# Small edits around the first LayerNorm and the first group of a fused attention and MLP layer

## The chip, the cores and the metric

The kernel runs on one core of one Trainium2 chip. The metric is the device time of one launch in microseconds (us). A core has five engines that run side by side and wait for one another on semaphores: TensorE (PE; its weight loads are shown apart as PEld), VectorE (DVE), ScalarE (ACT), GpSimd (POOL) and SyncE (SP), which here only issues DMAs.

## The reference

The layer is a pre-LayerNorm block on x of 2048 tokens by 576, in bfloat16. First a sliding, dilated attention with 32 heads of 18, where a token looks at itself and at the tokens 2, 4, ... 14 before it. Then an MLP, 576 to 4608 to 576. The MLP has a LayerNorm of its own on an input that was already normalized, so h passes two of them (the kernel folds both into one).

```python
def _A_ref(x, wqkv, wo):
    qkv = (x @ wqkv).reshape(B, S, 3, H, Dh) ...
    idx = pos[:, None] - off[None, :]        # off = 0, 2, .. 14
    logits = where(mask, einsum("bhsd,bhswd->bhsw", q, kg) * scale, -1e9)
    o = einsum("bhsw,bhswd->bhsd", softmax(logits), vg)
    return o.transpose(0, 2, 1, 3).reshape(B, S, D) @ wo
def _B_ref(x, w1, b1, w2, b2):
    return gelu(layernorm(x) @ w1 + b1) @ w2 + b2
h   = x + _A_ref(layernorm(x), A_wqkv, A_wo)
out = h + _B_ref(layernorm(h), B_w1, B_b1, B_w2, B_b2)
```

## The kernel before, in words

The 2048 tokens are 16 tiles of 128 rows. Row p of tile j is token 16p + j, so a window with a step of 2 stays among tiles of one parity, and a tile of earlier tokens is the same tile moved down by one row (a halo, read back from DRAM by `halo`, L335). Even tiles are treated first. The attention goes backwards, 14, 12, ... 0, then 15, 13, ... 1 (`ATT_ORDER`), and two neighbours in that order are a group: group 0 is tiles 14 and 12, group 1 is 10 and 8.

The order of each engine's work is written out by hand (`tc.manual_schedule`, L783): each engine executes its own instructions in the order of the program and waits where an operand isn't ready. Tables of calls say what follows which visit of TensorE.

- **Start** (L784 to L874). SP issues the loads of x and of the weights one after another. VectorE takes statistics of each tile and centres it (`ln1_even`, L834); the reciprocal root is a power on GpSimd (`ln_rstd`, L158). TensorE transposes the centred even tiles (`tr_x`, L265) with `transpose_in` (L177): products with an identity, for two halves of the rows, into two halves of a pair of banks. The 576 columns make four blocks of 128 and a rest of 64. The fifth block takes the last 128 columns. For LN1 that is enough, since other weights stand under it; for o and h (`twice`), the last 64 columns are transposed once more into the upper 64 rows, so that both halves of the fifth block hold them. That makes 12 products instead of 10. A copy turns the pair into xnT.
- **QKV stage** (L963). 24 visits of two products each (`visit`, L230, `phase`, L209). A phase does half of the contraction for each half of the array; before the second phase, a no-op on GpSimd (`marker`, L225) waits for the first one's last matmul, and the second phase waits for the no-op. Since GpSimd works in order, a marker is also held by whatever stands ahead of it there. ScalarE evacuates each product (`evac`, L308), from three pairs of banks in turn (`ring_pair`, L290). Odd tiles are normalized by ScalarE (`ln1_act`) and transposed by DMA through DRAM (`out_x`, `in_x`).
- **Attention** (L343 to L409) is VectorE's: products of q with eight shifted K tiles, a tree of adds, maximum, subtraction (`att_max`), exponential on ScalarE, and the same with V.
- **Output product and LN2.** o is transposed on TensorE for group 0 (`tr_o`, L422), by DMA for the others. `wo_duo` multiplies it with wo. `ln2_h` (L459) adds x on VectorE. For group 0 VectorE also takes the statistics (`ln2_more`), adds b2 (`add_b2`, L503) and works out the bias -mean * rstd (`ln2_bias`), and ScalarE normalizes (`ln2_hn`). For other groups ScalarE does all of it (`ln2_act`, `ln2_send`), b2 is put into x's place by a DMA (`put_b2`), and h is added to that by a DMA from GpSimd's queue (`accumulate_h`, L509). Their result is stored to DRAM and read back transposed (`ln2_in`, L497).
- **MLP** (L1005 on), group by group: `mlp1` with GELU on ScalarE, then `mlp2`. While group k is in the MLP, the attention of the next groups is on VectorE. Group 0's MLP starts when TensorE's last QKV visit is done. Inside group 0's `mlp2`, at rows 0 and 19 of its first tile (`ia[0]`, `ia[19]`), stand LN2 of group 1 and the scores of group 2.

The part around the table of calls that the change edits, in the kernel before:

```python
17: [c_(ln2, A[0]), c_(att_qk_a, A[2])],
18: [c_(ln2_rstd, A[0]), c_(add_b2, A[0]), c_(ln2_bias, A[0]), c_(halo, A[2], 1), c_(att_qk_add, A[2], ((0, 0, 9),))],
19: [c_(ln2, A[1])],
20: [c_(ln2_rstd, A[1]), c_(add_b2, A[1]), c_(ln2_bias, A[1]), c_(att_qk_rest, A[2], 0, 1)],
```

Of the kernel before, what the change touches and what calls it, by code (L numbers as in the profile page):

```python
# [17 lines left out]
def kernel(  # L18
# [69 lines left out]
    qp = qp_cm.__enter__()  # L88
    wq_sb = qp.tile([P, KF, 3 * D], BF16, name="wq_sb")
    wqh_sb = qp.tile([P, 3, D], BF16, name="wqh_sb")  # L90
    b2_bc = x_all[:, ODD[-1], :]

    kv_dram = dram.tile([NT, P + 1, 2, D], BF16, name="kv_dram")
    sync_dep = mybir.DependencyInfo(mybir.DependencyClass.Sync, mybir.DependencyReason.DATA)
# [46 lines left out]
    def ln_stats(srcs, tag, c1, c0, bufs, first=None, eps=True):  # L141
        n = len(srcs)
        pool = qp if tag.startswith("ln1") else sb
        stats = pool.tile([P, n, 2, nc.vector.BN_STATS_DIM], F32, tag=f"{tag}_stats", name=f"{tag}_stats", bufs=bufs)
        mv = pool.tile([P, n, nc.vector.BN_AGGR_DIM], F32, tag=f"{tag}_mv", name=f"{tag}_mv", bufs=bufs)
        for i, src in enumerate(srcs):
            for c in range(2):
                nc.vector.bn_stats(out=stats[:, i, c, :], in_=src[:, c * HALF:(c + 1) * HALF])  # L148
            nc.vector.bn_aggr(out=mv[:, i, :], in_=stats[:, i, :, :])
            if i == 0 and first is not None:  # L150
                first()
        if not eps:
            return mv, None
        veps = sb.tile([P, n], F32, tag=f"{tag}_veps", name=f"{tag}_veps", bufs=bufs)
        nc.vector.tensor_scalar(out=veps[:], in0=mv[:, :, 1], scalar1=c1, scalar2=c0, op0=ALU.mult, op1=ALU.add)  # L155
        return mv, veps
# [10 lines left out]
    def ln_bias(mean, rstd, tag, bufs):  # L167
        n = rstd.shape[1]
        nmr = sb.tile([P, n], F32, tag=f"{tag}_nmr", name=f"{tag}_nmr", bufs=bufs)
        nc.vector.scalar_tensor_tensor(out=nmr[:], in0=mean, scalar=-1.0, in1=rstd[:], op0=ALU.mult, op1=ALU.mult)  # L170
        return nmr
# [2 lines left out]
        nc.scalar.activation(out=dst, in_=src, func=ACT.Identity, scale=rstd, bias=nmr)  # L174


    def transpose_in(pair, src, twice=True):  # L177
        def turn(rows, kt, c):
            for r in range(2):
                block = src[half_rows(r), c:c + P if rows.start is None else D]  # L180
                nc.tensor.matmul(pair[rows, r, kt * HP:(kt + 1) * HP], lhsT=block, rhs=ident[half_rows(r), half_rows(r)],
                                 start=True, stop=True, skip_group_check=True)

        for kt in range(KT):
            turn(slice(None), kt, min(kt * P, D - P))
        if twice:
            turn(half_rows(0), KF, KF * P)
# [18 lines left out]
    def half_rows(r):  # L206
        return slice(r * HP, (r + 1) * HP)
# [56 lines left out]

    def tr_x(j, tag):  # L265
        pair = psum_pair(tag or "CAB"[(ring_pos[0] + 1) % 3], "xt_pt")
        transpose_in(pair, q_all[:, j, :], False)
        if EVEN.index(j) % 2 == 0:
            new_xnT(EVEN[EVEN.index(j):][:2])
        for k0, k1 in ((0, 2), (2, KT)) if j in EVEN[0:2] else ((0, KT),):  # L270
            copy = nc.vector.tensor_copy if j == EVEN[1] and k0 == 0 else nc.scalar.copy
            copy(**turned(xnT[j], pair, k0, k1))  # L272

    xd = [dram.tile([2, P, KT * P], BF16, name=f"xd{i}") for i in range(NT // 4)]

# [53 lines left out]
    def sides(js):  # L329
        return slice(side[js[0]], side[js[0]] + len(js))  # L330

    def logit_of(js):
        return logits[:, sides(js)]
# [27 lines left out]
            nc.vector.memset(out[0:1, j // 2 + 1:W, :], -1e9)  # L361

    def att_max(js):
        n, sl, lg = len(js), sides(js), logit_of(js)
        nc.vector.tensor_reduce(out=peak[:, sl], in_=lg.rearrange("p i w h -> p i h w"), axis=AX.X, op=ALU.max)
# [55 lines left out]

    def tr_o(j, tag):  # L422
        pair = psum_pair(tag, "o_pt")
        transpose_in(pair, q_all[:, j, :])
        nc.scalar.copy(**turned(new_oT(j), pair))

    def dma_tr_o(j):
# [24 lines left out]
    def x_of(j):  # L452
        return x_all[:, j - j % 2, :]
# [16 lines left out]

    def ln2_more(j):
        h = h_of[j]
        hn[j] = (h,) + ln_stats([h[:]], "ln2", 1.0 + EPS, EPS * EPS, 2)

    def ln2_act(j):
        h = h_of[j]
# [23 lines left out]
            tc.add_manual_dep(read[0], stored[0].name, sync_dep, reason="stores ahead of the transposes of LN2")  # L500
            stored[0] = None

    def add_b2(j):  # L503
        nc.vector.tensor_tensor(out=x_of(j), in0=h_of.pop(j)[:], in1=b2_bc, op=ALU.add)

    def put_b2(j):
        nc.sync.dma_start(out=x_of(j), in_=B_b2.partition_broadcast(P))

    def accumulate_h(j):  # L509
        ins = nc.gpsimd.dma_start(out=x_of(j), in_=h_of.pop(j)[:], accum_op=ALU.add).ins  # L510
        tc.add_manual_dep(ins, read[0].name, sync_dep, reason="behind the transposes of LN2")

    def ln2_rstd(j):
        h, mv, veps = hn[j]
# [2 lines left out]
    def ln2_bias(j):  # L517
        h, mv, rstd = hn[j]
        hn[j] = (h, rstd, ln_bias(mv[:, :, 0], rstd, "ln2", 2))

    def ln2_hn(j):
        h, rstd, nmr = hn[j]
# [8 lines left out]

    def tr_h(j, tag):
        pair = psum_pair(tag, "h_pt")
        transpose_in(pair, hn.pop(j)[:])
        nc.scalar.copy(**turned(hnT_slot(j), pair))

    def gelu_table():
# [143 lines left out]
    def c_(fn, *a):  # L681
        return lambda: fn(*a)
# [100 lines left out]
    with tc.manual_schedule(engines={ENG.PE, ENG.Activation, ENG.DVE, ENG.SP, ENG.Pool}):  # L783
# [9 lines left out]
        load_x(EVEN[3:4])  # L793
        load_wqkv(2, 2, KF)
        load_wqkv_tail(nc.sync, 2)
        for j in EVEN[4:8]:
            load(x_all[:, j:j + 2, :], x3[:, j:j + 2, :])
        load_x(ODD[0:2])
        load_x(ODD[2:4])
        load_wqkv(0, 0, 2)  # L800
        load_wqkv(0, 2, KF)
        load_wqkv_tail(nc.sync, 0)
# [113 lines left out]
        for n, v in enumerate((19, 19, 20, 20, 21, 22)):  # L916
# [3 lines left out]
            1: [c_(ln1_even_rstd, 2, 3), c_(ln1_even, 5)],  # L920
            2: [c_(ln1_even, 6), c_(ln1_even, 7), c_(ln1_even_rstd, 4, 5)],
            3: [c_(ln1_even_rstd, 6, 7), c_(ln1_stats, 8)],
            4: [c_(ln1_rstd, 8), c_(ln1_stats, 9), c_(ln1_stats, 10, c_(ln1_bias, 8))],
            5: [c_(ln1_act, 8, 0), c_(ln1_rstd, 9), c_(ln1_bias, 9), c_(att_qk_a, A[0])],
            6: [c_(ln1_rstd, 10), c_(ln1_act, 8, 1), c_(halo, A[0], 1), c_(out_x, 0)],
            7: [c_(att_qk_rest, A[0], 0), c_(ln1_bias, 10), c_(ln1_act, 8, 2), c_(in_x, 0)],
# [21 lines left out]
        wo_with = {17: A[0], 19: A[1]}  # L948
# [56 lines left out]
        for k, g in enumerate(GROUPS):  # L1005
# [123 lines left out]
```

## Time and profile before

| what | value |
|---|---|
| three runs of the kernel | 361.35, 362.5, 366.2 us (median 362.5) |
| the profiled execution: time, span | 361.35 us, 359.6 us |
| TensorE busy, granted clock | 353.4 us (98%), full |
| VectorE, ScalarE, GpSimd busy | 296.3, 234.8, 46.5 us |
| first transposes of x; first MLP matmul of group 0, of group 1 | 4.94; 66.55; 105.21 us |
| mean of a power for LN1 or LN2 statistics on GpSimd (L161) | 965 ns, 548 to 3007 |
| an accumulating DMA issued by GpSimd (L510) | 862 to 1547 ns of GpSimd |

The span is the profiled stretch of one execution; the time also has what lies around it. An engine is busy while an instruction runs on it. Matmuls are pipelined, so TensorE's busy time holds short stalls too; its waits and the distance of two starts say more. In a list of waits a row is "who waits <- for whom: total, times, longest", and a row of a timeline is start, length, engine, line, operation, output <- inputs, and in brackets the idle time ahead with what ended it.

### The profile page before, as it was taken

To read this page: it belongs to the slowest core of one execution; us is meant where nothing else is said; L and a number is where in the kernel's file an instruction comes from. 1 tells how busy PE (TensorE), PEld (TensorE's weight loads), DVE (VectorE), ACT (ScalarE), POOL (GpSimd) and SP (SyncE) were. 2 spreads that over 40 slices of the span, in tenths; PEclk is the share of its full clock that TensorE was granted. 3 is DMA by queue.
4 is the path that set the end of the run, shared out by engine and by line. 5 is a ranking of instruction groups with operands and counts; after the bars stand their busy time and mean duration, and the time that the engine had idled before them with its cause. 6 is when DMAs were issued, how large, how long until landed. Compare 5 with 4: busy or idle time off the path is not lost.

```text
span 359.6 us, 11560 instructions
## 1 busy us (share of the span) xinstructions
PE 353.4 (98%) x4942; PEld 292.4 (81%) x4942; DVE 296.3 (82%) x417; ACT 234.8 (65%) x519; POOL 46.5 (13%) x61
## 2 busy tenths in 40 slices
PE   7999999999999999999999999999999999999996
PEld 3778977887789877887788778877887788778874
DVE  5999999999989999997799899989998998520431
ACT  4879756897647783668566956695669566706620
POOL 2241004000112020201110202021102110210000
PEclk9999999999999999999999999999999999999999
DMA  7996789973447494731563655344636254273001
GB/s 241 339 285 192 202 223 300 369 246 73 136 88 119 142 239 81 137 71 51 94 101 76 98 124 85 90 96 110 88 90 100 57 86 58 54 122 50 4 1 33
DMA packets 62980, 46.29 MB, mean 129 GB/s; under 512 B 32192, under 2 KB 60736, under 8 KB 62928
## 3 DMA queue, kind: packets, MB, share of 16 engines
q1 hardware_dynamic: 58960, 41.50, 44.0%
q0 software_dynamic: 3744, 3.84, 9.8%
q8 instruction: 38, 0.62, 0.8%
q10 hardware_dynamic: 224, 0.22, 0.2%
q14 instruction: 14, 0.11, 0.1%
HBM read 23.38 MB, written 12.42 MB: 100 GB/s over the span
## 4 chain that ended last, share of the span: by engine, by line
PE 76%; DVE 14%; DMA 3%; SPq 2%; ACT 2%; issue 1%; POOL 0%; POOLq 0%; ACTq 0%
PE pm L216 34%; PE po L669 25%; PE pq L216 8%; PE po L581 5%; PE pw L216 4%; DVE prod L352 2%; DVE ln_stats L148 2%; DVE prod L343 2%; DVE prod L398 1%; DMA x_all<-in_A_x_dram 1%; DVE prod L404 1%; ACT h_all L562 1%; SPq L104 1%; DMA hnT<-td 1%; DMA oT<-td 1%
## 5 line engine op out<-in xcount | busy, mean ns | idle before, releaser
L216 PE MATMUL pm<-hnT,w_sb 64*128 64x256 bf16 x2304 | 143.0, 269 | 0.2 <-DMA hnT<-td 0.2
L562 ACT ACTIVATE h_all<-pm,b_sb 128x256 f16<-128x256 f32 (+1 forms) x288 | 108.6, 496 | 51.2 <-PE pm L216 50.6
L216 PEld LDWEIGHTS <-w_sb 64*128 64x128 bf16 x2304 | 113.6, 94 | 13.5 <-issue 1.9
L669 PEld LDWEIGHTS <-h_all 128*128 128x128 f16 x480 | 46.2, 98 | 13.7 <-issue 1.6
L216 PE MATMUL pq<-wq_sb,xnT 64*128 64x288 bf16 x720 | 54.9, 283 | 1.3 <-ACT xnT L272 0.5
L216 PEld LDWEIGHTS <-xnT 64*128 64x128 bf16 x864 | 44.0, 94 | 10.6 <-ACT xnT L272 1.2
L352 DVE TENSOR_TENSOR prod<-prod 128x2304 bf16<-128x2304 bf16 (+1 forms) x64 | 44.2, 691 | 2.0
L343 DVE TENSOR_TENSOR prod<-kv_ring,q_all 128x4608 bf16<-128x4608 bf16 x16 | 40.9, 2555 | 3.1 <-POOL ln_rstd L482 2.5
L398 DVE TENSOR_TENSOR prod<-kv_ring,probs 128x4608 bf16<-128x4608 bf16 x16 | 40.9, 2558 | 1.1 <-DMA kv_ring<-kv_dram 0.6
L216 PE MATMUL pm<-hnT,w1h_sb 64*128 64x256 bf16 x288 | 39.5, 269 | 0.0
L669 PE MATMUL po<-w2a_sb,h_all 128*128 128x288 bf16 (+1 forms) x262 | 35.8, 286 | 0.0
L404 DVE TENSOR_TENSOR prod<-prod 128x2304 bf16<-128x2304 bf16 (+1 forms) x32 | 33.9, 1058 | 1.1
L581 PEld LDWEIGHTS <-h_all 128*128 128x128 bf16 x288 | 27.9, 98 | 7.9 <-issue 1.0
L669 PEld LDWEIGHTS <-kv_ring 128*128 128x128 f16 x252 | 24.6, 98 | 6.3
L581 PE MATMUL po<-w2a_sb,h_all 128*128 128x288 bf16 x224 | 28.5, 286 | 0.0
L216 PE MATMUL pq<-wqh_sb,xnT 64*128 64x288 bf16 x144 | 27.6, 283 | 0.0
L771 POOL DMA_DIRECT2D x_all<-o_sb x12 | 10.7, 890 | 124.6 <-PE pw L216 71.8
L482 POOL TENSOR_TENSOR ln_rstd<-ln_var,mhalf 128x1 f32<-128x1 f32 x13 | 9.3, 718 | 81.9 <-ACT ln_var L481 81.9
L669 PE MATMUL po<-w2b_sb,h_all 128*128 128x288 bf16 (+1 forms) x122 | 19.7, 286 | 0.2 <-DVE h_all L649 0.2
L649 DVE TENSOR_TENSOR kv_ring<-h_all 128x1536 f16<-128x1536 f16 (+3 forms) x9 | 6.8, 761 | 15.6 <-ACT h_all L562 15.6
L216 PE MATMUL pw<-wo_sb,oT 64*128 64x288 bf16 x256 | 19.5, 283 | 0.1
L161 POOL TENSOR_TENSOR ln_rstd<-ln_veps,mhalf 128x1 f32<-128x1 f32 (+2 forms) x14 | 13.3, 965 | 47.6 <-DVE ln_veps L155 31.1
(107 smaller groups left out, 399.3 us busy)
## 6 DMA issues: line engine op xcount, KB each, us to landing
w_sb<-in_B_w_dram SPq DMA_DIRECT2D x6, 768.0 KB, 6.3
kv_ring<-kv_dram SPq DMA_DIRECT2D x28, 144.0 KB, 2.4
kv_dram<-kv_ring SPq DMA_DIRECT2D x13, 288.0 KB, 4.1
x_all<-in_B_b_dram SPq DMA_DIRECT2D x15, 144.0 KB, 3.7
w2a_sb<-in_B_w_dram SPq DMA_DIRECT2D x2, 1008.0 KB, 8.0
td<-q_all SPq DMA_DIRECT2D x14, 144.0 KB, 1.8
td<-hn SPq DMA_DIRECT2D x14, 144.0 KB, 1.8
x_all<-h POOLq DMA_DIRECT2D x14, 144.0 KB, 4.8
```

Source lines behind the costliest of these rows:

```text
L148: nc.vector.bn_stats(out=stats[:, i, c, :], in_=src[:, c * HALF:(c + 1) * HALF])
L161: nc.gpsimd.tensor_tensor(out=rstd[:], in0=veps[:], in1=mhalf[:].to_broadcast([P, n]), op=ALU.pow)
L216: last = nc.tensor.matmul(duo["g"][r ^ swap][i], lhsT=lhsT, rhs=rhs, start=(swap == 0 and i == 0 and kt == 0), stop=(swap == 1 and kt == K ...
L343: ins = nc.vector.tensor_tensor(out=prod[:], in0=k_ring[j % 2], in1=q_all[:, j, :].unsqueeze(1) .to_broadcast([P, W, D]), op=ALU.mult).ins
L352: nc.vector.tensor_tensor(out=prod[:, :, o * H:o * H + n], in0=prod[:, :, a * H:a * H + n], in1=prod[:, :, c * H:c * H + n], op=ALU.add)
L398: nc.vector.tensor_tensor(out=prod[:].rearrange("p w (d h) -> p w d h", h=H), in0=v_ring[j % 2].rearrange("p w (d h) -> p w d h", h=H), in ...
L404: nc.vector.tensor_tensor(out=prod[:, 0:n, :], in0=prod[:, 0:n, :], in1=prod[:, n:2 * n, :], op=ALU.add)
L482: ins = nc.gpsimd.tensor_tensor(out=rstd[:], in0=var[:], in1=mhalf[:], op=ALU.pow).ins
L562: pace[0] = nc.scalar.activation(out=hT(grp)[:, f, 0:N], in_=ps[:, r, i * N:(i + 1) * N], func=ACT.Gelu_apprx_tanh, bias=b1_sb[:, f:f + 1] ...
L581: nc.tensor.matmul(banks[half], lhsT=hT(grp)[:, f, i * P:(i + 1) * P], rhs=w2_rows(f)[:, half * HALF:(half + 1) * HALF], start=(f == 0), s ...
L669: nc.tensor.matmul(bank, lhsT=l, rhs=r, start=start, stop=stop, skip_group_check=True)
L771: nc.gpsimd.dma_start(out=x_of(j), in_=o_of.pop(j), accum_op=ALU.add)
```

## The change

- **Loads.** Even tiles 8 to 14 were loaded in pairs with their odd neighbours, four loads; now 8 alone, 10 and 12 together, 14 alone, and the odd tiles in two loads of four.
- **xnT.** The copy of the first two blocks of the second even tile moves from VectorE to ScalarE.
- **LN1 bias.** The bias of the first four odd tiles is worked out ahead of the last statistics, not between them.
- **o tails.** ScalarE copies the last 64 columns of o twice side by side into a tile, so that the fifth transpose of `tr_o` gives both halves: 10 products, not 12. The transposes of h keep their 12.
- **LN2 of group 0.** VectorE negates the mean; ScalarE multiplies it with rstd ahead of the normalization (`ln2_norm`). b2 is put into x's place by DMA and h is accumulated onto it by GpSimd's DMA, behind the first visit of the MLP.
- **Group 1 and 2 inside group 0's `mlp2`.** The subtraction after the maximum of tile 6 comes after the second h on VectorE; the two transposing reads of hn are issued one by one, the first ahead of the second's sends, and the halo read of tile 4 behind both; two halo stores come earlier.

```diff
-    b2_bc = x_all[:, ODD[-1], :]
...
-    def transpose_in(pair, src, twice=True):
...
+    def transpose_in(pair, src, tail=None):
+        for kt in range(KT):
+            c = min(kt * P, D - P)
+            block = src[:, c:c + P] if kt < KF or tail is None else tail
             for r in range(2):
...
+    def transpose_tail(pair, src):
...
+    def o_tail(j):
+        o_tails[j] = qp.tile([P, 2, HP], BF16, tag="tail", name="tail", bufs=2)
+        nc.scalar.copy(out=o_tails[j][:], in_=q_all[:, j, KF * P:D].unsqueeze(1).to_broadcast([P, 2, HP]))
...
-            copy = nc.vector.tensor_copy if j == EVEN[1] and k0 == 0 else nc.scalar.copy
-            copy(**turned(xnT[j], pair, k0, k1))
+            nc.scalar.copy(**turned(xnT[j], pair, k0, k1))
...
     def att_max(js):
+        att_peak(js)
+        att_less(js)
...
     def ln2_more(j):
         h = h_of[j]
-        hn[j] = (h,) + ln_stats([h[:]], "ln2", 1.0 + EPS, EPS * EPS, 2)
+        mv, veps = ln_stats([h[:]], "ln2", 1.0 + EPS, EPS * EPS, 2)
+        if j in GROUPS[0]:
+            nmean = sb.tile([P, 1], F32, tag="ln2_nmean", name="ln2_nmean", bufs=2)
+            nc.vector.tensor_scalar(out=nmean[:], in0=mv[:, 0, 0:1], scalar1=-1.0, scalar2=None, op0=ALU.mult)
+            mv = nmean
+        hn[j] = (h, mv, veps)
...
-    def add_b2(j):
-        nc.vector.tensor_tensor(out=x_of(j), in0=h_of.pop(j)[:], in1=b2_bc, op=ALU.add)
...
     def accumulate_h(j):
         ins = nc.gpsimd.dma_start(out=x_of(j), in_=h_of.pop(j)[:], accum_op=ALU.add).ins
-        tc.add_manual_dep(ins, read[0].name, sync_dep, reason="behind the transposes of LN2")
+        if read[0] is not None:
+            tc.add_manual_dep(ins, read[0].name, sync_dep, reason="behind the transposes of LN2")
...
+    def ln2_norm(j):
+        h, nmean, rstd = hn[j]
+        nc.scalar.activation(out=nmean[:], in_=nmean[:], func=ACT.Identity, scale=rstd[:, 0:1])
+        hn[j] = (h, rstd, nmean)
+        ln2_hn(j)
...
-        for j in EVEN[4:8]:
-            load(x_all[:, j:j + 2, :], x3[:, j:j + 2, :])
-        load_x(ODD[0:2])
-        load_x(ODD[2:4])
+        load_x(EVEN[4:5])
+        load_x(EVEN[5:7])
+        load_x(EVEN[7:8])
+        load_x(ODD[0:4])
+        load_x(ODD[4:8])
...
-            4: [c_(ln1_rstd, 8), c_(ln1_stats, 9), c_(ln1_stats, 10, c_(ln1_bias, 8))],
+            4: [c_(ln1_rstd, 8), c_(ln1_stats, 9), c_(ln1_bias, 8), c_(ln1_stats, 10)],
...
-            14: [c_(att_pv, A[1]), c_(in_x, 3), c_(load, b2_bc, B_b2.partition_broadcast(P))],
-            15: [c_(halo, A[1], 2)],
-            17: [c_(ln2, A[0]), c_(att_qk_a, A[2])],
-            18: [c_(ln2_rstd, A[0]), c_(add_b2, A[0]), c_(ln2_bias, A[0]), c_(halo, A[2], 1), c_(att_qk_add, A[2], ((0, 0, 9),))],
+            14: [c_(att_pv, A[1]), c_(in_x, 3)],
+            15: [c_(halo, A[1], 2), c_(o_tail, A[0])],
+            17: [c_(o_tail, A[1]), c_(ln2, A[0]), c_(att_qk_a, A[2])],
+            18: [c_(ln2_rstd, A[0]), c_(put_b2, A[0]), c_(halo, A[2], 1), c_(att_qk_add, A[2], ((0, 0, 9),))],
             19: [c_(ln2, A[1])],
-            20: [c_(ln2_rstd, A[1]), c_(add_b2, A[1]), c_(ln2_bias, A[1]), c_(att_qk_rest, A[2], 0, 1)],
+            20: [c_(ln2_rstd, A[1]), c_(put_b2, A[1]), c_(att_qk_rest, A[2], 0, 1)],
...
-            19: [c_(ln2_hn, A[0])],
-            21: [c_(ln2_hn, A[1])],
+            19: [c_(ln2_norm, A[0])],
+            21: [c_(ln2_norm, A[1])],
...
-                m1[1] = [c_(pv_t, c), c_(pv_t, d), c_(att_qk_a, e), c_(halo, e, 1)]
+                m1[1] = [c_(accumulate_hs, *g), c_(pv_t, c), c_(pv_t, d), c_(att_qk_a, e), c_(halo, e, 1)]
...
-                ia[0] = [c_(ln2_h, c), c_(ln2_act, c), c_(put_b2, c), c_(ln2_send, c), c_(att_qk_rest, e, 0)]
-                ia[19] = [lambda d=d: wo_visit((d, "A"), fill=True), c_(ln2_h, d), c_(ln2_act, d), c_(put_b2, d), c_(att_qk_a, f),
-                          c_(halos, 2), c_(halo, f, 1), c_(ln2_send, d), c_(ln2_ins, c, d), c_(att_qk_rest, f, 1), c_(exps, e, f)]
+                ia[0] = [c_(ln2_h, c), c_(ln2_act, c), c_(put_b2, c), c_(halos, 2), c_(ln2_send, c), c_(att_qk_b, e, 0), c_(att_peak, [e])]
+                ia[19] = [lambda d=d: wo_visit((d, "A"), fill=True), c_(ln2_h, d), c_(ln2_act, d), c_(put_b2, d), c_(ln2_in, c),
+                          c_(att_less, [e]), c_(att_qk_a, f), c_(ln2_send, d), c_(ln2_in, d), c_(halo, f, 1), c_(att_qk_rest, f, 1),
+                          c_(exps, e, f)]
```

More of the change, by code (lines that the diff above doesn't have):

```diff
@@ L174, in ln_apply_act @@
         nc.scalar.activation(out=dst, in_=src, func=ACT.Identity, scale=rstd, bias=nmr)
-    def transpose_in(pair, src, twice=True):
-        def turn(rows, kt, c):
+    def transpose_in(pair, src, tail=None):
+        for kt in range(KT):
+            c = min(kt * P, D - P)
+            block = src[:, c:c + P] if kt < KF or tail is None else tail
             for r in range(2):
[L180 to L187, printed above, removed]
+                nc.tensor.matmul(pair[:, r, kt * HP:(kt + 1) * HP], lhsT=block[half_rows(r)],
+                                 rhs=ident[half_rows(r), half_rows(r)], start=True, stop=True, skip_group_check=True)
+    def transpose_tail(pair, src):
+        for kt in range(KF):
+            for r in range(2):
+                nc.tensor.matmul(pair[:, r, kt * HP:(kt + 1) * HP], lhsT=src[half_rows(r), kt * P:(kt + 1) * P],
+                                 rhs=ident[half_rows(r), half_rows(r)], start=True, stop=True, skip_group_check=True)
+        for c, rows in ((D - P, slice(None)), (KF * P, half_rows(0))):
+            for r in range(2):
+                nc.tensor.matmul(pair[rows, r, KF * HP:KT * HP], lhsT=src[half_rows(r), c:c + P if rows.start is None else D],
+                                 rhs=ident[half_rows(r), half_rows(r)], start=True, stop=True, skip_group_check=True)
+    o_tails = {}
+    def o_tail(j):
+        o_tails[j] = qp.tile([P, 2, HP], BF16, tag="tail", name="tail", bufs=2)
+        nc.scalar.copy(out=o_tails[j][:], in_=q_all[:, j, KF * P:D].unsqueeze(1).to_broadcast([P, 2, HP]))
     def turned(dst, pair, k0=0, k1=KT):
@@ L266, in tr_x @@
         pair = psum_pair(tag or "CAB"[(ring_pos[0] + 1) % 3], "xt_pt")
-        transpose_in(pair, q_all[:, j, :], False)
+        transpose_in(pair, q_all[:, j, :])
         if EVEN.index(j) % 2 == 0:
@@ L363, in att_max, with att_peak, att_less @@
     def att_max(js):
+        att_peak(js)
+        att_less(js)
+    def att_peak(js):
+        sl, lg = sides(js), logit_of(js)
+        nc.vector.tensor_reduce(out=peak[:, sl], in_=lg.rearrange("p i w h -> p i h w"), axis=AX.X, op=ALU.max)
+    def att_less(js):
         n, sl, lg = len(js), sides(js), logit_of(js)
-        nc.vector.tensor_reduce(out=peak[:, sl], in_=lg.rearrange("p i w h -> p i h w"), axis=AX.X, op=ALU.max)
         nc.vector.tensor_tensor(out=lg, in0=lg, in1=peak[:, sl].unsqueeze(2).to_broadcast([P, n, W, H]), op=ALU.subtract)
@@ L423, in tr_o @@
         pair = psum_pair(tag, "o_pt")
-        transpose_in(pair, q_all[:, j, :])
+        transpose_in(pair, q_all[:, j, :], o_tails.pop(j)[:].rearrange("p r c -> p (r c)"))
         nc.scalar.copy(**turned(new_oT(j), pair))
@@ L533, in tr_h @@
         pair = psum_pair(tag, "h_pt")
-        transpose_in(pair, hn.pop(j)[:])
+        transpose_tail(pair, hn.pop(j)[:])
         nc.scalar.copy(**turned(hnT_slot(j), pair))
```

## The prediction

> **What bounds the kernel now.** I read the page first, then the table by stage (busy time of each engine in stretches I chose), then TensorE's waits, then the timelines around each wait.
>
> ```profile
> span 359.6 us, 11560 instructions
> PE 353.4 (98%) x4942; PEld 292.4 (81%) x4942; DVE 296.3 (82%) x417; ACT 234.8 (65%) x519; POOL 46.5 (13%) x61
> PEclk9999999999999999999999999999999999999999
> ...
> 10.00:24.00 14.00, 13.72 (x268) 10.77 (x266) 13.21 (x50) 11.23 (x18) 4.89 (x8) 1.00 1.07 324
> 24.00:45.00 21.00, 20.74 (x337) 18.80 (x335) 20.22 (x28) 18.70 (x31) 3.01 (x1) 1.00 0.70 202
> 57.00:66.50 9.50, 9.35 (x166) 7.47 (x164) 8.71 (x18) 7.61 (x13) 1.09 (x2) 1.00 1.05 374
> 125.50:339.00 213.50, 213.50 (x2888) 177.93 (x2888) 173.97 (x213) 138.31 (x329) 27.84 (x34) 1.00 0.49 91
> ```
>
> TensorE is the bound in every stage and its granted clock is full. From 125.5 to 339 us, untouched by the change, it has no idle time. So the change can win only what TensorE's own small waits before 125.5 and two groups of transposes are worth; work taken off VectorE counts only through those. The waits, TensorE's weight loads (PEld) first:
>
> ```profile
> PEld L216 <- ACT xnT L272: 1.2, 3, 0.6
> PEld L181 <- DVE q_all L826: 1.2, 3, 0.5
> PEld L216 <- DMA oT<-td: 1.0, 3, 0.4
> PEld L216 <- POOLq L226: 0.7, 2, 0.4
> PE pq L216 <- ACT kv_ring L311: 0.2, 1, 0.2
> PE pm L216 <- DMA hnT<-td: 0.2, 1, 0.2
> ```
>
> Each is a few tenths: columns are total, times, longest. The timelines of TensorE, ScalarE and GpSimd give the places that decide:
>
> ```profile
> 45.87 0.48 PE L181 MATMUL o_pt<-ident,q_all 64*128 64x64 bf16 x12
> 46.28 0.66 PE L216 MATMUL pq<-wq_sb,xnT 64*128 64x288 bf16 x7
> ...
> 58.90 0.67 PE L216 MATMUL pq<-wq_sb,xnT 64*128 64x288 bf16 x8
> 62.96 0.46 PE L181 MATMUL h_pt<-ident,hn 64*128 64x64 bf16 x12
> ...
> 57.45 0.87 ACT L174 ACTIVATE hn<-h,ln_nmr,ln_rstd 128x576 bf16<-128x576 f32 x1 [0.83 <-DVE ln_nmr L170]
> 58.22 1.17 ACT L311 ACTIVATE kv_ring<-pq 128x576 bf16<-128x576 f32 x2
> 61.45 0.65 ACT L311 ACTIVATE kv_ring<-pq 128x576 bf16<-128x576 f32 x1
> 62.00 0.86 ACT L174 ACTIVATE hn<-h,ln_nmr,ln_rstd 128x576 bf16<-128x576 f32 x1
> ...
> 54.28 2.80 POOL L161 TENSOR_TENSOR ln_rstd<-ln_veps,mhalf 128x1 f32<-128x1 f32 x1 [26.40 <-DVE ln_veps L155]
> 60.71 1.00 POOL L161 TENSOR_TENSOR ln_rstd<-ln_veps,mhalf 128x1 f32<-128x1 f32 x1 [3.62 <-DVE ln_veps L155]
> ```
>
> The reader is to see two things. ScalarE's evacuations are just in time: the first of the pair at 58.22 ends near 58.86 and TensorE takes a freed bank at 58.90 (three pairs of banks go round); the second normalization ends at 62.86 and its transposes start at 62.96. And the power on GpSimd takes 2.80 us beside VectorE's 2.55 us product, 1.00 us otherwise.
>
> **The change, part by part.** I follow S, how much earlier than now TensorE stands, through the program.
>
> *Loads and first copy.* VectorE's LN1 is gapless from 10.62, when the load of the fifth even row landed (issued 5.79, 4.80 us). It brings that row and an odd one, 288 KB; afterwards 144 KB. At the 362 GB/s of 6.5 to 10 us that is 0.41 us less; the other end is 0, if the last of the sixteen engines is late anyway. I take 0.4. VectorE no longer waits 1.00 us and copies 0.42 us for xnT, so it is ready for that row. Smaller rows cost transfer time at most in the odd loads, which are needed only from 16.5 us; cover gone, each 0.1 us late there is 0.1 us on VectorE. ScalarE's second pair of xnT copies starts at 7.27 instead of 7.73 but has one piece more: 0.1 to 0.2 us, swallowed at the next wait. TensorE's wait at 16.4 is on VectorE's centring: **S = 0.4**.
>
> *LN1 bias earlier.* It frees ScalarE's 0.59 us wait at 23.66 and so TensorE's 0.24 us at 25.20. But at 35.8 TensorE waits for the odd rows' transposing DMA (0.3), queued on SP behind a halo read that waits for VectorE's product ending at 27.3, and that is only 0.4 earlier. S stays 0.4.
>
> *Tails.* Twelve transposes take 46.28 - 45.87 = 0.41 us, the last two on 64 rows of output costing the difference; ten take 0.15 (xt_pt, 12.53 to 12.68). Twice 0.26. ScalarE adds two copies of 128x128: between 128x36 (0.19) and 128x256 (0.41), 0.29 by interpolation; the first must follow VectorE's last add at 45.62, gives 0.03 of its saving back, and the second lies in a 1.6 us idle stretch. [...] The second transposes start only when VectorE has read the bank (h, 52.92), 0.4 earlier. **S = 0.66**.
>
> *LN2 of group 0.* Off VectorE: two adds of 0.67 net, two biases of 0.07 and the 0.45 wait for the power at 61.75; on it, two 0.07 negations: 1.8 us net, 2.2 with the 0.4. None of it helps the first normalization: the power still sits beside the product, 0.4 - 0.07 earlier; ScalarE then scales the mean, 0.33 us with its gap (row 91.57, 0.29), where it now waits for the bias until 57.45. So hn, the evacuation behind it and TensorE at 58.90 come 0.33 earlier: **S falls to 0.33**. TensorE's wait for a marker held in GpSimd's queue behind the second power (60.75) goes, as VectorE is 1.0 earlier there: +0.22. Then the new 0.33 stands between the evacuation at 61.45 and hn, and TensorE has only 0.1 slack at 62.96: **S = 0.12**. The ends: -0.2 if the power, now beside VectorE's adds, is late; +0.55 if the scaling hides.
>
> *DMAs.* SP issues as many as before (two b2 loads more; the old b2 load and one x load fewer). Each b2 load waits until VectorE has read its row of x for h: about 52.5 and 58, while SP, by its rows of today, reaches them near 55 and 60. Behind them stand a halo read that waits for VectorE's product until 56.3 anyway and the w2 loads (0.35 to 0.5 us of SP for each b2 load), unused before 85.7; if h were late, those would be late by as much. GpSimd gets two accumulates, 0.86 to 1.55 each, behind the first visit's markers: in the next group they begin 3.1 us after the stage starts and take 1.77 together. The next marker is needed 6.1 us after the start (a visit of 3.9 and the next one's first phase of 2.2, pm from 66.55), so 1.2 us is left: nothing on the path.
>
> *Second h and reads.* VectorE's 2.2 us bring the first oT early: TensorE's wait at 83.6 goes, +0.23. At the second h VectorE now waits for TensorE (92.4), so only 0.6 of its lead is left; h ahead of the 0.42 subtraction and the reads no longer behind the halo hide the hnT wait at 105.21: +0.26. The read of the first hnT is moved ahead of the sends (1.2 us of SP), which wait for ScalarE anyway; the halo read goes behind both and is used 14 us later. At 123.76 TensorE waits 0.25 for oT, whose chain of products starts 0.6 earlier: S ends at min(0.86, 0.65) = **0.65**.
>
> The profiled execution took 361.35 us (span 359.6 and 1.75 around it): 361.35 - 0.65 = **360.7**. It is also the fastest of three runs; their median lies 1.15 higher at 362.5, and the third is 366.2.
>
> **Rivals.** *All waits close.* If ScalarE's slack is larger than its rows say, 0.4 (load) + 0.4 (bias) + 0.2 (copy) + 0.2 (odd rows) + 0.5 (tails) + 0.2 (marker) + 3 x 0.25 (oT, hnT, oT) = 2.65 pass through: 358.7. For it: each is seen. Against: the evacuation ending at 58.86 for a start at 58.90.
>
> *The power is held by the adds.* The second power, started near 59.6, would run beside three adds (1.47 together) and the logits' add (0.42), and end at 61.9 instead of about 60.7; hn and TensorE come 0.3 later than now, the later waits give back 0.3 to 0.5: 361.2. For it: 2.80 against 1.00 us. Against: 0.67 beside an add at 90.86. [...]
>
> *Slower: the accumulates block GpSimd's queue.* If each is held through a product of 2.56 us as the power was, two take 6.9 us; begun 3.1 after the stage's start they end at 10.0, and TensorE's marker, needed at 6.1, stalls it 3.9: 364.6. It decides once the two take over 3.0 us, or b2 lands later than 72 us. Against: 1.77 beside products at 108.32. [...]
>
> **How the numbers follow.** Forecast 0.50, all waits close 0.20, power held 0.20, accumulates 0.05, 0.05 for what I don't see. The likeliest time is 360.7 for a run like the profiled one; its own range is 360 to 362. The whole range reaches down to the first rival, 358.6, and up past the power rival by the 1.15 to the median and a little of the third run: 363.6. Two per cent, about what a measurement here tells from no change, is 7 us; no case reaches it: faster 0.02, within 0.95, slower 0.03.
>
> **What would show it.** Right: VectorE's first statistics after a load wait at about 10.2; o_pt rows x10 of 0.3 us; TensorE's waits for POOLq near 60, hnT at 105 and oT at 83 gone; h_pt of the second tile waiting for ScalarE; pm beginning 0.1 earlier than 66.55 and po of the second group 0.65 earlier than 125.46. Wrong: pm beginning a microsecond earlier (ScalarE didn't gate), or TensorE waiting for POOLq between 68 and 80 (accumulates).

## The result, and the profile after

The changed kernel takes 364.75 us (median of 22, 362.11 to 367.7), the kernel before on the same chips 362.03 (median of 22): a ratio of 1.0058, 95% interval 1.0034 to 1.0083. That is within 2 per cent, but the interval lies wholly on the slower side, and the median lies above the predicted range, which ended at 363.6. The slowest execution, 367.7, lies over 1.5 per cent above the fastest of its kernel and is left out of the ratio. The profiled execution took 365.63 us with a span of 363.9, against 361.35 and 359.6 before.

From its page, the span and the 40 slices of 9.1 us: in the tenth, 82 to 91 us, TensorE is busy only 6 tenths, and its clock is not full.

```profile
span 363.9 us, 11557 instructions
...
PE   7998999996999999999999999999999999999996
...
PEclk9999999998999999999999999999999999999999
```

TensorE's waits from 5 to 130 us. The wait for oT, 0.4 at the longest before, is 2.9 in one place, and the odd rows' xnT costs 1.0; the one for hnT is gone:

```profile
PE pw L227 <- DMA oT<-td: 3.3, 2, 2.9
PE pq L227 <- DMA xnT<-xd: 1.0, 1, 1.0
```

The table by stage of the changed kernel (start and end, length, busy time of PE, PEld, DVE, ACT, POOL, granted clock, share of DMA, GB/s):

```profile
74.00:78.00 4.00, 4.00 (x79) 3.56 (x76) 3.86 (x6) 3.96 (x10) 0.00 (x0) 1.00 1.10 232
78.00:82.00 4.00, 4.00 (x78) 3.66 (x74) 0.46 (x2) 3.90 (x11) 0.00 (x0) 1.00 0.89 300
82.00:86.00 4.00, 1.51 (x28) 1.17 (x24) 3.02 (x2) 3.03 (x8) 0.00 (x0) 0.97 0.22 46
86.00:90.00 4.00, 3.63 (x36) 2.42 (x37) 3.90 (x4) 0.56 (x2) 0.00 (x0) 0.60 0.30 80
```

and of the kernel before:

```profile
74.00:78.00 4.00, 4.00 (x78) 3.57 (x74) 3.93 (x3) 3.96 (x10) 0.00 (x0) 1.00 0.88 296
78.00:82.00 4.00, 4.00 (x78) 3.66 (x74) 3.86 (x6) 3.92 (x11) 0.00 (x0) 1.00 0.18 53
```

Before, the DMA engines are done with the weights at 76 to 77 us (53 GB/s from 78 on). After, they are full until about 81, and from 74 to 78 they are full at 232 GB/s (392 from 70 to 74): that is where the two accumulates run. VectorE then does 0.46 us of work in four, and TensorE's 82 to 86 is more than half empty. The chain of waits of the changed kernel, in order of time (start, length, what), leads from one to the other:

```profile
77.56 5.90 DMA td<-q_all
...
83.48 2.84 DMA oT<-td
...
86.36 1.38 PE pw L227 x10
```

The o of the second group is sent to DRAM (td) and read back transposed (oT), and TensorE waits at the read's end. The DMA issues of 66 to 90 us (KB each, median us from issue to landing) show that these small transfers became slow, not late; of the changed kernel:

```profile
kv_ring<-kv_dram SPq DMA_DIRECT2D x3, 144.0 KB, 8.2
...
td<-q_all SPq DMA_DIRECT2D x2, 16.0 KB, 5.9
```

and of the kernel before:

```profile
kv_ring<-kv_dram SPq DMA_DIRECT2D x4, 144.0 KB, 2.8
...
td<-q_all SPq DMA_DIRECT2D x2, 16.0 KB, 1.6
```

The store of o was in fact issued earlier than before, at 77.56 against 79.21. The halo reads of 8.2 us, against 2.8, are also why VectorE stood still: its next product began at 82.94 after 4.45 us of waiting for one. And TensorE, when oT came, was slow for some 3 us (timeline):

```profile
86.36 1.14 PE L227 MATMUL pw<-wo_sb,oT 64*128 64x288 bf16 x8 [2.86 <-DMA oT<-td]
...
89.23 0.65 PE L227 MATMUL pw<-wo_sb,oT 64*128 64x288 bf16 x8
89.81 3.36 PE L607 MATMUL po<-w2a_sb,h_all 128*128 128x288 bf16 x26
```

Eight matmuls of pw take 1.14 at 86.36 and 0.65 at 89.23; the same shape. From the first of these matmuls to the first of po are 3.45 us, and 2.08 before.

Where the 4.3 us of the two spans lie, by the starts of the same instructions:

| start of (us) | before | after | later by |
|---|---|---|---|
| MLP of group 0 (pm) | 66.55 | 66.53 | 0.0 |
| Wo product of the next group (pw) | 83.60 | 86.36 | 2.8 |
| group 0's second product (po) | 85.68 | 89.81 | 4.1 |
| MLP of group 1 (pm) | 105.21 | 109.09 | 3.9 |
| group 1's second product (po) | 125.46 | 129.73 | 4.3 |
| end of the span | 359.57 | 363.86 | 4.3 |

The medians differ by less, 2.7: of the 21 executions that the ratio compares, eleven have a mean granted clock of at most 0.995 (the profiled one has 0.995) and a median of 365.35; ten have 0.998 or more, and 363.08. A stretch of 3 us at half clock is 0.004 of the mean, so the ten can hardly have had a whole one; the loss behind the wait seems to vary from execution to execution.

### The profile page after: what moved, and what is told of

It reads as the page before. It is cut to its first block, busy times and chain, and to the rows that moved or that the text cites. A ratio compares the mean times of both kernels' runs of the same rounds, so it can differ in the third digit from the quotient of the medians.

```text
span 363.9 us, 11557 instructions
## 1 busy us (share of the span) xinstructions
PE 353.8 (97%) x4938; PEld 291.1 (80%) x4938; DVE 294.7 (81%) x414; ACT 235.9 (65%) x524; POOL 48.6 (13%) x63
## 4 chain that ended last, share of the span: by engine, by line
PE 74%; DVE 11%; DMA 9%; ACT 2%; SPq 2%; issue 1%; DVEq 0%; ACTq 0%
PE pm L227 34%; PE po L695 25%; PE po L607 10%; PE pw L227 4%; DVE ln_stats L147 3%; DMA kv_ring<-kv_dram 3%; DVE prod L353 2%; DMA oT<-td 2%; DMA td<-q_all 2%; DMA xnT<-xd 2%; DVE prod L415 1%; DMA x_all<-in_A_x_dram 1%; DVE prod L421 1%; SPq L103 1%; PE pq L227 1%; ACT h_all L588 1%
## 5 line engine op out<-in xcount | busy, mean ns | idle before, releaser
L227 PEld LDWEIGHTS <-w_sb 64*128 64x128 bf16 x2304 | 112.2, 94 | 15.4 <-issue 1.7
L415 DVE TENSOR_TENSOR prod<-kv_ring,probs 128x4608 bf16<-128x4608 bf16 x16 | 40.9, 2558 | 6.4 <-DMA kv_ring<-kv_dram 5.9
L353 DVE TENSOR_TENSOR prod<-kv_ring,q_all 128x4608 bf16<-128x4608 bf16 x16 | 40.9, 2556 | 3.0 <-POOL ln_rstd L504 2.4
L227 PEld LDWEIGHTS <-oT 64*128 64x128 bf16 x288 | 14.1, 96 | 7.8 <-DMA oT<-td 3.9
```

The source lines that it names most:

```text
L227: last = nc.tensor.matmul(duo["g"][r ^ swap][i], lhsT=lhsT, rhs=rhs, start=(swap == 0 and i == 0 and kt == 0), stop=(swap == 1 and kt == K ...
L353: ins = nc.vector.tensor_tensor(out=prod[:], in0=k_ring[j % 2], in1=q_all[:, j, :].unsqueeze(1) .to_broadcast([P, W, D]), op=ALU.mult).ins
L415: nc.vector.tensor_tensor(out=prod[:].rearrange("p w (d h) -> p w d h", h=H), in0=v_ring[j % 2].rearrange("p w (d h) -> p w d h", h=H), in ...
```

## The experiments

The theory to test: the two b2 loads and the two accumulates, 144 KB each, are put into a stretch in which weights keep the DMA engines full (shares of 1.03 to 1.08 in each four us from 58 to 74 us before); the backlog ends later, and the small transfers on the way to oT wait in it. Rivals: an issue order that holds something on SP or GpSimd, the other five parts of the change, or VectorE's lead (it is up to 1.65 us earlier than before and so asks for its transfers while the engines are still full). Each experiment was timed beside the kernel before on the same chip.

**Without the DMA form of b2.** The changed kernel, with VectorE's addition and its one load of b2 as before:

```diff
-c_(put_b2, A[0])   ...   c_(put_b2, A[1])
+c_(add_b2, A[0])   ...   c_(add_b2, A[1])
-m1[1] = [c_(accumulate_hs, *g), c_(pv_t, c), ...
+m1[1] = [c_(pv_t, c), ...
```

> The changed kernel with b2 of group 0 added by VectorE again, as before (no b2 loads into x's place, no accumulates of group 0; the other edits stay). Theory (traffic): the two b2 loads and two accumulates lengthen the stretch in which the DMA engines are saturated with weights (57 to 77 us before), a halo read and the store of o wait behind it, TensorE waits 2.9 us for oT and then runs at half clock for a while. So here that wait is gone (under 0.4 us), the clock stays full, and the time is 0.2 to 1.0 us below the kernel before. Rival (loads): the smaller loads of x and the earlier LN1 are to blame by shifting the whole queue; then the wait for oT stays over 2 us and the time stays 2 us above before. Rival (lead): VectorE's lead alone moves its requests into the backlog; here a lead of 0.4 us is left, so under it some 0.3 us of the wait would stay.

Measured: 362.41 us, ratio 1.0020 (1.0005 to 1.0034), span 359.9. The oT wait is gone, so the loss hangs on this part. But the gain foreseen for the other parts did not come: this kernel is not faster than before. Its largest new wait is

```profile
PE pq L228 <- POOLq L238: 0.8, 1, 0.8
```

which ends at 61.11 us: a marker of TensorE stands behind the second power in GpSimd's queue.

**The DMA form of b2 alone,** put into the kernel before (`add_b2` becomes `put_b2`, and the accumulates are issued behind the first visit of the MLP):

> The kernel before with one edit: b2 of group 0 by DMA loads and accumulates instead of VectorE's adds (bias and all else as before). Traffic: this alone brings the late halo read, a wait of TensorE for oT of 1.5 to 3 us near 84 us and 1.5 to 4 us more time than before. Loads: no wait, time within 0.5 us of before. Lead: VectorE is only 1.3 us earlier here, so the wait is some 0.8 us shorter than in the changed kernel, about 2 us.

Measured: 365.43 us, ratio 1.0110 (1.0085 to 1.0136), span 364.2. This part alone costs more than the whole change, and its profile has the same places: a wait of 3.3 us for oT and a clock of 0.58 from 86 to 90 us. VectorE's lead is only 0.6 us in this kernel (td sent at 78.63, before at 79.21), and yet the wait is longer: the lead doesn't make it.

**The accumulates two visits later** in the changed kernel, the b2 loads where they are:

```diff
-m1[1] = [c_(accumulate_hs, *g), c_(pv_t, c), ...
+m1[3] = [c_(accumulate_hs, *g)]
+m1[1] = [c_(pv_t, c), ...
```

> The changed kernel with the two accumulates of group 0 moved from ahead of the second visit of the MLP to ahead of its fourth (near 78 us); the b2 loads stay. If the accumulates' slow transfers (192 to 240 GB/s on all queues while they run, against 390) are most of the lengthening, the backlog ends 2 us or more earlier, the halo read of 74.7 lands before 79.5, the wait for oT is under 1 us, the clock stays full and the time is 361 to 362.5. If the lead or the b2 loads are enough by themselves, the wait stays near 2.9 us and the time above 364. If accumulates near 80 us hold the store and read of oT instead, a wait of 1 to 2 us stays.

Measured: 361.62 us, ratio 0.9998 (0.9986 to 1.0009), span 359.8. Of the waits for oT half a microsecond is left, and the transfers of 66 to 90 us lie between the two kernels:

```profile
td<-q_all SPq DMA_DIRECT2D x2, 16.0 KB, 3.6
```

So the long wait hangs on the accumulates being in that stretch. The loads that stayed are no small rest of the backlog, though: the engines are full until about 78.5 us here, 76 to 77 before and 81 in the changed kernel, and VectorE still waits 2.2 us for the halo read.

**Less of the other traffic.** The changed kernel with the last load of W2, 1152 KB, issued on SP behind the two transposing reads of oT, at 88.56 us, instead of in the MLP's first visit at 69.39:

> The changed kernel with the last load of w2 (1152 KB, some 3 us of all DMA engines at 385 GB/s) moved on SP from ahead of the halo read to behind the second transposing read of oT; b2 by DMA stays. Both traffic and lead: the backlog is over before VectorE asks, the wait for oT is gone, the clock stays full, and the time is 0.3 to 1.2 us below the kernel before. Loads: wait and time stay as in the changed kernel. A new wait is possible if the moved load lands after TensorE's row 28 of the first tile, near 93 us: then po waits for w2b.

Measured: 362.71 us, ratio 1.0026 (1.0013 to 1.0039), span 360.3. With the accumulates where the change puts them, the oT wait is gone too, with VectorE still further ahead (td sent at 76.85). So it is the sum of the traffic that decides, not the accumulates as such. A new wait came in its place, for the load that was put off:

```profile
PE po L607 <- DMA w2b_sb<-in_B_w_dram: 1.5, 1, 1.5
```

**Loads and accumulates both late.** The b2 loads behind the third visit, the accumulates behind the fourth:

```diff
+m1[2] = [c_(put_b2, g[0]), c_(put_b2, g[1])]
+m1[3] = [c_(accumulate_hs, *g)]
```

> The changed kernel with both b2 loads of group 0 moved from the busy stretch before 66 us to behind the third visit of that group's MLP, and its accumulates to behind the fourth, so that nothing of the new DMA traffic lies in the stretch in which the weights fill the DMA engines. Traffic theory: the oT wait at 83 to 86 us falls from 2.9 to at most 0.2, no slow stretch of TensorE follows it, the second group's products start at 83.0 to 83.6 (before: 83.60), and the time is 0.2 to 0.6 us below the kernel before: 361.1 to 361.5 where before has 361.7. Rival (the other parts give nothing, or cost what they give): the wait goes as well, but the time is within 0.2 us of before, 361.5 to 361.9, or above it.

Measured: 375.32 us, ratio 1.0357 (1.0315 to 1.0400), span 373.5: a miss of both theories, and the worst kernel of all. TensorE waits once, and GpSimd's timeline says for what:

```profile
PE pm L227 <- POOLq L237: 11.6, 1, 11.6
```

```profile
91.59 1.05 POOL L529 DMA_DIRECT2D x_all<-h  x1 [30.93 <-DMA x_all<-in_B_b_dram]
```

The loads stood in SP's queue behind the sending and the transposing read of the second o and a halo read, which follow VectorE's work, and were issued at 87.72. The accumulate waited for the load in GpSimd's queue, and behind it stood the marker that TensorE needs between the halves of a visit. This is the prediction's slower rival, by its second condition (b2 landing later than 72 us), in a kernel that nobody meant. TensorE's clock is 0.50 from 86 us, still inside the wait, to 98, five us behind its end.

**Three parts alone, in the kernel before.** First the early part (loads of x, first xnT copy, LN1 bias):

> The kernel before with the early part alone: the loads of x cut as in the change, ScalarE copying all of the first xnT, and the LN1 bias ahead of the third odd row's statistics. The prediction's step: TensorE 0.4 us earlier at the last transposes of x (16.0 instead of 16.40) and 0.4 earlier all the way to the end: 0.4 us below the kernel before. Rival, from the changed kernel's trace: earlier by about 0.5 at 16 us, but all of it lost at 35.8, where TensorE waits for the transposing DMA of the odd rows (longest wait 1.0 instead of 0.3), since that DMA comes no earlier; the time within 0.15 us of before.

Measured: 362.11 us, ratio 0.9999 (0.9973 to 1.0026). The rival holds for the median: TensorE's wait for the odd rows' transposing DMA at 35 us, 0.3 before, is 0.8 now and takes back what was won.

Then the o tails:

> The kernel before with the o tails alone: two ScalarE copies of 128x128, and ten transposes instead of twelve for each of the two o tiles. The prediction's step: the transposes take 0.15 instead of 0.41 us; the first time 0.23 of it is kept, the second time the start waits for the bank anyway; TensorE 0.2 us earlier at 60 us and the time 0.1 to 0.3 below before. Rival: each tail copy of 0.30 us holds the evacuation behind it on ScalarE, the gain is given back at the next bank that TensorE takes, and the time is within 0.1 of before or above it.

Measured: 362.02 us, ratio 0.9991 (0.9968 to 1.0014); no difference that can be told. The saving itself is there, as the changed kernel's timeline shows (from the first transpose at 45.87 us to the next product 0.15 us, 0.41 before), but not in the time.

Then the order of the second group's LN2:

> The kernel before with the order of the second group's LN2 alone: the second h ahead of the subtraction of the softmax, the halo reads moved, and each read of hnT placed by itself. The prediction's step: the hnT wait at 105.21 (0.2 to 0.26) goes and nothing else changes: second group's MLP 0.2 us earlier, time 0.1 to 0.3 below before. Rival: moving the halo reads and the subtraction makes the chain of products for the next group late by as much, and the gain is given back at the oT wait of 123.76 (0.25 becomes 0.4 to 0.5): within 0.1 of before.

Measured: 361.58 us, ratio 0.9974 (0.9952 to 0.9996): a gain of about 0.9 us, more than foreseen. In its profile, group 1's MLP begins 21.36 us after the Wo product (21.61 before) and its second product 20.00 after that (20.25), so both places of the prediction gave 0.25, without the loss that the rival expected. The same profile lost 0.7 in a place that the edit doesn't touch. VectorE's sum of h and b2 waited for b2:

```profile
57.05 0.76 DVE L511 TENSOR_TENSOR x_all<-h,x_all 128x576 bf16<-128x576 f32 x1 [0.71 <-DMA x_all<-in_B_b_dram]
```

This load is as near to late in the kernel before: issued at 52.82 and landed 3.6 us later, for a sum at 56.59.

**Tails and order together,** in the kernel before:

> The kernel before with two parts alone, the o tails and the order of the second group's LN2: no new DMA traffic, no scaling by ScalarE, loads as before. If small gains add up: 0.25 of the hnT wait at 105, 0.25 of the oT wait at 123 and up to 0.2 of the tails, together 0.5 to 0.7 us below the kernel before. Rival: a gain in one place is taken by the next transfer that was just in time (LN2's b2 sum waiting for its load at 56 us, as in the run with the order alone, 0.7 us), and the time lies within 0.3 us of before.

Measured: 361.43 us, ratio 0.9978 (0.9963 to 0.9992), 0.8 us below: the first theory's gain, but no more than the order gives alone.

**The changed kernel without its whole LN2 part of group 0** (b2 and the bias by VectorE as before):

> The changed kernel without its whole LN2 part of group 0: b2 added by VectorE and the LN2 bias by VectorE, as before; early loads, tails and the order of the second group are the change's. Against the variant that kept ScalarE's bias (0.2 per cent above before, with 0.8 us of TensorE's wait for GpSimd's queue at 60 us and hn behind the scaling): if the bias by ScalarE costs 0.3 to 0.6, this one comes 0.1 to 0.4 us below before (odd rows' transposing DMA still takes the early gain). Rival: the bias costs nothing and the loss lies in the early part: then this one too is 0.3 to 0.9 above before.

Measured: 362.24 us, ratio 0.9994 (0.9979 to 1.0009). Against the 1.0020 of the kernel with ScalarE's bias the intervals overlap, so ScalarE's bias may cost some 0.9 us or nothing; and beside the 0.9978 without the early part, the early part costs rather than gives, which is not sure either. The profiled execution, 364.0 us, is the longest of its twelve, and its loss is the b2 load again: VectorE waited 1.76 us for it at 57 us, TensorE then 1.9 for an evacuation.

**The clock by itself.** The changed kernel, with twelve products of constants in front of the Wo product, in the bank that it then overwrites:

```diff
             pw = psum_pair(tag, "pw")
             t = oT.pop(j)
+            if j == GROUPS[1][0]:
+                for _ in range(12):
+                    nc.tensor.matmul(pw[:, 0, 0:512], lhsT=ones[:, 0:P], rhs=ones[:, 0:512], start=True, stop=True)
```

> The changed kernel with twelve matmuls on constants, 128x512 into the bank of the first product with Wo, put into TensorE's queue where it waited 2.9 us for oT at 83 us; the product overwrites them. 12 at 0.21 us at full clock are 2.56 us, so TensorE's idle time falls to about 0.4 and oT comes no earlier. Clock theory (the idle time halves the clock for 3 us behind it, 235 instead of 120 ns a pair): the half clock goes, the second group's first product with W2 (89.81 in the changed kernel) starts at about 88.4, and the time falls by 1.4 us, to 1.0 to 1.6 above the kernel before. Rival (the half clock comes of the full DMA or of the work behind the wait, not of the idle time): still 2.3 to 3.3 above before, pitch still 235 ns.

Measured: 364.32 us, ratio 1.0060 (1.0038 to 1.0082). The timeline:

```profile
83.61 2.79 PE L461 MATMUL pw<-const-bfloat16-1.0 128*128 128x512 bf16 x11
86.85 0.66 PE L227 MATMUL pw<-wo_sb,oT 64*128 64x288 bf16 x8 [0.46 <-DMA oT<-td]
...
88.94 3.24 PE L610 MATMUL po<-w2a_sb,h_all 128*128 128x288 bf16 x25
```

The half clock hangs on the idle time, as the first theory has it (clock 1.00 from 86 to 90 us, 0.60 in the changed kernel): oT comes 0.5 later than in the changed kernel's profile, and the second product starts 0.87 earlier, since the eight matmuls take 0.66 at once (1.14 there) and the stretch from pw to po 2.09 (3.45 there). The gain in time is not shown: at 1.0060 beside 1.0058 nothing is won on the median, a miss of the 1.4 us expected. A likely reason, not tested, is that the filler takes its time (2.79 us in the profile for the eleven matmuls recorded, where 2.56 was expected for twelve) in every execution, also where the wait would be shorter or the clock would hold.

**A version that beats both?** Tails and order in the kernel before, and the one b2 load put into another free row and issued at 47.7 us instead of 52.8:

```diff
-    b2_bc = x_all[:, ODD[-1], :]
+    b2_bc = x_all[:, ODD[0], :]
...
-            13: [c_(ln1_act, 10, 1), c_(in_x, 2), c_(out_x, 3)],
-            14: [c_(att_pv, A[1]), c_(in_x, 3), c_(load, b2_bc, B_b2.partition_broadcast(P))],
+            13: [c_(ln1_act, 10, 1), c_(in_x, 2), c_(out_x, 3), c_(load, b2_bc, B_b2.partition_broadcast(P))],
+            14: [c_(att_pv, A[1]), c_(in_x, 3)],
```

> The variant with tails and order alone (0.22 per cent below the kernel before) with one more edit: the single b2 load of group 0, which in the kernel before is issued at 52.8 us and lands 0.2 us ahead of its first use at 56.6 (in three variants it landed 0.6 to 1.8 late), goes into another free row of x and is issued some 4.5 us earlier, before a load of W1 and ahead of a 3 us wait of SP. Just-in-time theory: VectorE's wait for that load is gone for good, and the time is at or below the variant's: 0.2 to 0.5 per cent below the kernel before (360.4 to 361.5 where that has 362.2). Rival (the late loads of those runs were noise that costs nothing on the median, or the moved load only shifts the wait to the W1 load or the odd rows' transposing DMA behind it): 0.0 to 0.2 per cent below.

Measured: 361.00 us, ratio 0.9982 (0.9969 to 0.9994), span 358.8. It is faster than both kernels, by 0.7 us than the one before. Its profile has no late b2 load, and TensorE waits nowhere longer than 0.6 up to 130 us, but its ratio is that of the variant without the moved load: that the late b2 cost the median anything is not shown.

## Why the prediction was wrong

**The step that failed** is "*DMAs* ... nothing on the path". It counted the new DMAs as issue time on SP and GpSimd, and asked only who stands behind them in those two queues. It never asked how long they hold the DMA engines, though its own stage table had them at a share of 1.05 before group 0's MLP. What the runs put in its place: a stretch that was full until 76 to 77 us gets two loads and two accumulates of 144 KB in place of one load that had landed at 56.4, stays full until 81, and everything small behind it is late. The store td takes 5.9 us instead of 1.6, the halo reads 8.2 instead of 2.8, and TensorE starts on oT 2.8 later. In the traces, what SP issues isn't free of what GpSimd issues: a store that SP issued took 5.9 us with the accumulates of GpSimd ahead of it, and 3.6 with these issued later.

**Most of its size could have been worked out beforehand.** The queues of the kernel before (packets, MB, time of the packets as a share of the sixteen engines' span):

```profile
q1 hardware_dynamic: 58960, 41.50, 44.0%
q0 software_dynamic: 3744, 3.84, 9.8%
```

GpSimd's queue (q0), which carries accumulates alone, takes 9.8% of 359.6 us for 3.84 MB, 9.2 us a MB; SP's (q1) takes 3.8. Two accumulates of 0.147 MB are 2.7 us of all engines, and two b2 loads at 385 GB/s (62 to 66 us before) 0.8: an estimate of 3.5 us more backlog. Measured in the changed kernel, 72 to 78 us:

```profile
GB/s 392 384 415 399 376 392 470 376 392 369 399 353 407 338 277 200 215 238 200 207 192 192 223 207 154 238 238 169 192 184 223 177 192 192 215 238 292 392 369 369
...
q1 hardware_dynamic: 1126, 1.41, 68.0%
q0 software_dynamic: 286, 0.29, 40.9%
```

The accumulates are 40.9% of 6 us, 2.5 us, and while they run all queues together move about 200 GB/s. The loads cost more than their bytes. In the stretch where they run the kernel before moves 374 GB/s (row of 57 to 66.5 us in the prediction), the changed one 328:

```profile
57.00:66.50 9.50, 9.23 (x160) 7.31 (x156) 8.93 (x16) 7.96 (x15) 1.00 (x1) 1.00 1.01 328
```

That is 0.4 MB less, 1.1 us at 390 GB/s; with the loads moved away (the late b2 loads above), one slice of the page, 56.0 to 65.4 us, has 354, as in the kernel before, and 326 in the changed one. So the estimate is 2.5 + 0.8 + 1.1 = 4.4 us of backlog, and the end of the full stretch moved from 76 to 77 us to 81. Of this TensorE sees 2.9, since before, the engines had been free for some 2 us when td was sent. That the wait hangs on the accumulates is shown by moving them, and that the total decides, by moving W2 instead. No run takes the loads alone away, so the split between loads and accumulates is worked out, not shown.

**Left out altogether:** every stall in the prediction costs its own length. Behind 2.9 us of idle time TensorE's clock is 0.60 over the next 4 us, and the same work takes 1.4 us more; with the gap filled it doesn't (2.09 us from pw to po, against 3.45). A wait of 3.3 us (b2 by DMA alone) was followed by 0.58 over the same stretch; the single waits of 1.5 (W2 late) and 1.9 (b2 late) left the clock at 1.00 in the stage they lie in.

**The slower rival** (the accumulates block GpSimd's queue, 364.6) came within 0.2 us of the median by luck, by another mechanism. The accumulates themselves took 1.97 us of GpSimd, near the 1.77 of the forecast, and no marker waited between 66 and 100 us. An accumulate can block that queue, as the kernel with late b2 loads shows, there by waiting for its load; but in the changed kernel it didn't happen.

**The rest, point by point.** *Loads:* right in place (last transposes of x at 15.83, 16.40 before), though the first transposes alone start between 4.80 and 5.14 in these runs. *LN1 bias:* wrong that 0.4 is kept: the wait for the odd rows' transposing DMA ended at 35.81 as before, and S, the lead, was 0 there. The step named that DMA and let it start earlier by the lead. It did, at 30.07 instead of 30.68, but took 5.7 us instead of 5.1; why is not known. *Tails:* each set of transposes is 0.26 shorter as forecast, but the second set starts only 0.15 earlier (52.82, before 52.97), where 0.4 was forecast. *LN2 of group 0:* right in the mechanism. ScalarE gates, and the second power isn't held by adds (2.86 us beside the product, 1.00 at 60.01), so the rival at 361.2 falls. S came out at 0.02 where MLP 0 starts, forecast 0.12. *Tail copy:* 0.30 us; the estimate from the rows was 0.29. *Second h and reads:* right, the hnT wait went, and alone this part is worth 0.26% (0.04 to 0.48). In the changed kernel the second oT was late again near 127 us, by 0.64 us (0.26 before).

**What stays open.** Where the oT wait is gone or short, the change comes out at 0.9998 (accumulates late) and 1.0020 (without the DMA form), and 0.65 us less would be 0.9982. The profiles show three places that take the gain (the odd rows' DMA, ScalarE's scaling ahead of hn, a b2 load just in time), and the last of them, 0.6 to 1.8 us in three of the profiles, 0.3 in one and 0 in others, varies by more than the parts are worth. It can't be the reason in the kernel with late accumulates, which has no such load. Which of them takes the gain in the median isn't settled.

## What to carry to other kernels

A DMA had two prices here, its issue on a queue (1.97 us of GpSimd for two accumulates) and its bytes on the sixteen engines (2.5 us for the same two). In a stretch with a DMA share of 1.10 the second was paid by small transfers that something waited for (td 5.9 us instead of 1.6). So add new traffic only where the table by stage shows room, and price an accumulate by its own queue's us per MB. Where the trace shows a load moving fewer bytes than its neighbours, price that too. Ask of each DMA that an engine's own queue waits on what stands behind it: an accumulate put behind a late load cost 11.6 us. And where several waits were just in time, a gain ahead of one was taken by it (with the early part alone, TensorE's wait at 35 us rose from 0.3 to 0.8); time the parts alone before adding up their tenths.

## What the runs showed of the hardware

- In the changed kernel, 72 to 78 us, two accumulates of 144 KB into SBUF held the DMA engines, by the time of their packets, about three times as long a byte as the other traffic of the same stretch: 40.9% of 6 us for 0.29 MB against 68.0% for 1.41 MB, 8.5 and 2.9 us a MB; the total fell from some 390 to some 200 GB/s.
- A 16 KB store issued into a full stretch took 5.9 us where the engines stayed full for 3.4 us after its issue, and 1.6 where they were at a share of 0.18.
- In the profiled executions an idle time of TensorE of 2.9 us was followed by some 3 us at half clock (0.60 over 4 us), one of 1.5 or 1.9 us by none (1.00 over the 4 us it lies in). In an idle time of 11.6 us the clock fell to 0.50 before it ended and stayed there for 5 us after it.
